# Two buffers for the replaced maxima of a top-k chain, three operand buffers for the mixture layers, and a new table of order

## Chip, cores and metric

One core of a Trainium2 chip runs the whole program. The metric is the device time of one execution in microseconds, as the median of several runs; less is better. The kernel before takes 1180.86 us (median of 3 runs, 1180.18 to 1182.09).

## What is computed

Attention in which each row keeps its 32 largest scores, and behind it two mixture-of-experts layers, all in float32. Cut to what matters:

```python
# q, k, v: (4, 8, 576, 64)
scores = q @ k.T / 8                      # per batch and head: 576 x 576
kth    = the 32nd largest score of a row
scores = where(scores >= kth, scores, -1e9)
attn   = exp(scores - max) / (sum + 1e-9)
x      = (attn @ v), heads side by side   # (2304, 512)
h      = maximum(x @ w_in1, 0)            # (2304, 2048)
x      = (h * h) @ w_out1                 # (2304, 512)
h      = x @ w_in2
out    = (h * clip(h + 3, 0, 6) / 6) @ w_out2
```

## The kernel before

**Tiles.** The 2304 rows are cut, batch by batch, into four blocks of 128 rows and one of 64. A block has eight tiles, one for each head (the block of 64 rows has four, of two heads each, so that they too fill 128 rows). That makes 144 tiles `s` of 128 x 576 scores. `attend(s)` builds the chain of one tile: the scores on TensorE (`qk`, L767, into the one PSUM buffer `s`), their copy to SBUF by ScalarE (`evac`, L773, into one of three buffers `S`), the top-k on VectorE, one bias and the limit (`lowest`, L798), then `below` on ScalarE (L803), `mask` on GpSimd (L806), `expo` on ScalarE (L811), the split of the weights into two float16 parts (`high` L817 on ScalarE, `low` L821 and L822 on GpSimd), a transposing DMA (`flip`), and the product with v on TensorE (`av`, L840, 14 matmuls for a tile). The buffer `S` comes free when `mask` has read it; the next `evac` into that buffer is that of tile `s` + 3.

**The top-k chain.** Seven steps `topk(0)` to `topk(6)` on VectorE: a MAX8 over `S` (L781) gives the eight largest; then three times a MATCH_REPLACE8 (L786) replaces the eight just found by -3e38 and a MAX8 (L789) takes the next eight. The first MATCH_REPLACE8 reads `S` and writes the buffer `W`, the others read and write `W`, and the MAX8s between read `W`. On the chip each MATCH_REPLACE8 is two instructions, of which a MATCH_VALUE_LOAD of the eight values comes first. Each step reads what the step ahead of it wrote. There is one buffer `W`: it is taken by `topk(1)` and comes free behind `topk(6)`, so the next tile can do no more than its first MAX8 until then.

**Mixture layers.** `x_operand(i)` scales and splits a finished block into an operand `hl`; a unit `u` is a block of 128 rows, or two blocks of 64, 18 units in all. For each unit `group(m, u, g)` does, for layer m = 0 and 1 and four groups g: 12 matmuls `up` (L1080), a relu on ScalarE (L1086 or L1088), a square (L1091) or on VectorE a gate (L1094), a split (L1099 on ScalarE, L1102 on GpSimd), a transposing DMA, and 12 matmuls `acc` (L1114). That is 3456 matmuls of 512 columns. The buffer `hl` of a unit is taken by the copy out of PSUM (L912) and comes free behind the last `up` of layer 1; there are four.

**Weights.** Each of the four matrices comes in 16 slabs as 64-bit floats. `w_convert` makes 32-bit ones of them on VectorE (L362 to L365), ScalarE (L408) and GpSimd (L412), TensorE multiplies each slab with itself for a norm (`gram`, L428), and `w_split` splits them in two float16 parts over TensorE and ScalarE (L536 to L545) or ScalarE and GpSimd (L518 to L524). No `up` can start before its matrices are split.

**Order.** Nothing is scheduled at run time: `Plan` writes one list for each engine, and each engine works through its list in order, waiting at the head. `Plan.run` walks through a model of the engines, and whenever an engine is free it takes, of the tasks that are ready and whose buffers are to be had, the one with the smallest key `offset + slope * position`, from the table `PRIO` (L1285 to L1392). So each number of the table, each latency and each buffer count can move instructions on all engines.

Of the kernel before, what the change touches and what calls it, by code (L numbers as in the profile page):

```python
# [9 lines left out]
F32 = mybir.dt.float32  # L10
# [9 lines left out]
P = 128  # L20
# [12 lines left out]
class Plan:  # L33
# [7 lines left out]
    def pool(self, **sizes):  # L41
        for name, n in sizes.items():
            self.pools[name] = list(range(n))
# [91 lines left out]
def tile_topk_attention_moe_moe2(  # L135
# [12 lines left out]
    B, H, S, D = q.shape  # L148
# [40 lines left out]
    def pool(name, n, shape, dtype, where=None):  # L189

        plan.pool(**{name: n})
        size[name] = (shape, dtype, where or sb)
# [20 lines left out]
    acc_t = ps.tile([P, 2, 512], F32, name="acc")  # L213
    plan.pool(acc0=1, acc1=1)
    pool("S", SBUFS, [P, S], F32)
    pool("W", 1, [P, S], F32)
    pool("E", 2, [P, S], F32)
    pool("wc", 2, [P, 2 * S], F16)
    pool("wT", WTB, [P, 2 * S // P, P], F16)
# [6 lines left out]
    pool("f", FBUFS, [P, 512], F32)  # L226
    pool("hl", HBUFS, [P, 2, KD, P], F16)
    pool("ghl", GBUFS, [P, 2, 512], F16)
# [1025 lines left out]
def first_of(order, b):  # L1254
# [6 lines left out]
SBUFS = 3  # L1261
FBUFS = 2
XBUFS = 1
HBUFS = 4
GBUFS = 3
PREFILL = 1
SKV = 'd'
# [15 lines left out]


PRIO = {  # L1285
    "load0": (471.21, 0.193),
    "load1": (618.10, 5.848),
    "load2": (925.04, 0.019),
    "load3": (-584.22, 0.593),
    "conv0": (-88.95, 0.627),  # L1290
    "bits0": (361.28, 2.911),
    "add0": (4977.17, 0.028),
    "gram0": (-831.79, 0.031),
    "conv1": (-93.08, 4.311),
    "bits1": (41.48, 36.796),
    "add1": (368.64, 13.688),
    "gram1": (4879.36, 6.367),
    "conv2": (-80.47, 2.054),
    "bits2": (398.55, 0.019),
    "add2": (449.95, 4.070),  # L1300
    "gram2": (927.27, 0.037),
    "conv3": (-37.62, 1.038),
    "bits3": (-32.80, 0.358),
    "add3": (298.46, 0.239),
    "gram3": (338.67, 0.648),
    "norm": (-1082.21, 0.048),
    "high0": (71.90, 0.086),
    "low0": (72.95, 1.006),
    "scaled0": (205.37, 0.095),
    "rest0": (306.08, 0.054),  # L1310
    "high1": (406.08, 0.677),
    "low1": (-169.41, 49.252),
    "scaled1": (-407.57, 38.073),
    "rest1": (-988.86, 0.160),
    "high2": (983.60, 0.068),
    "low2": (-52.38, 0.243),
    "scaled2": (196.72, 28.830),
    "rest2": (336.50, 0.508),
    "high3": (313.76, 0.250),
    "low3": (-250.55, 0.031),  # L1320
    "scaled3": (307.88, 1.559),
    "rest3": (17.56, 2.177),
    "qsquare": (30.31, 2.898),
    "qtotal": (430.60, 4.982),
    "qscale": (-275.30, 0.171),
    "ksquare": (423.72, 0.406),
    "ktotal": (372.77, 1.000),
    "kscale": (-89.11, 1.034),
    "vsquare": (-201.56, 15.782),
    "vtotal": (-148.39, 5.232),  # L1330
    "vscale": (202.69, 1.991),
    "clear": (4572.71, 0.037),
    "kload": (-15.56, 1.826),
    "vload": (158.91, 2.703),
    "qload": (128.87, 1.164),
    "qhigh": (-47.12, 0.379),
    "qlow": (180.10, 0.411),
    "khigh": (110.60, 0.063),
    "klow": (88.64, 0.053),
    "vhigh": (-0.62, 3.120),  # L1340
    "vlow": (-617.68, 5.745),
    "kflip": (-880.94, 4.825),
    "qscales": (26.46, 0.807),
    "qflip": (39.22, 0.226),
    "qk": (-80.19, 0.810),
    "evac": (-83.75, 1.084),
    "topk": (299.98, 1.000),
    "bias": (-78.63, 7.605),
    "lowest": (300.78, 1.000),
    "below": (-0.40, 4.373),  # L1350
    "mask": (-1424.47, 1.367),
    "expo": (810.67, 1.170),
    "whigh": (-1146.93, 0.851),
    "wlow": (5245.85, 6.690),
    "wflip": (418.75, 3.778),
    "av": (-596.66, 1.207),
    "xinv": (-93.91, 1.674),
    "xscales": (340.01, 0.011),
    "xcopy": (4297.66, 2.864),
    "xflip": (-39.76, 7.585),  # L1360
    "xsquare": (136.44, 0.290),
    "xtotal": (28.37, 7.283),
    "xscale": (146.77, 0.924),
    "xevac": (-46.31, 0.145),
    "xhigh": (-43.97, 0.023),
    "xlow": (-85.79, 0.020),
    "common": (-820.64, 2.732),
    "ysquare": (307.25, 1.077),
    "ytotal": (613.31, 0.179),
    "yflip": (100.03, 2.762),  # L1370
    "yscale": (-497.39, 1.399),
    "yhigh": (330.72, 0.486),
    "ylow": (-206.35, 4.143),
    "whole": (-480.52, 0.870),
    "up0": (4592.97, 2.379),
    "up1": (5118.98, 5.912),
    "relu0": (919.05, 20.673),
    "relu1": (7.31, 2.302),
    "gsquare": (-112.41, 0.730),
    "gate": (109.54, 0.960),  # L1380
    "ghigh0": (83.10, 1.657),
    "ghigh1": (-853.86, 1.145),
    "gflip0": (374.33, 1.182),
    "gflip1": (-496.46, 1.917),
    "glow0": (-26.68, 0.590),
    "glow1": (76.85, 0.449),
    "acc0": (124.81, 0.498),
    "acc1": (788.57, 3.038),
    "oscale": (-125.90, 0.041),
    "oevac": (-4.66, 3.434),  # L1390
    "store": (-2145.32, 6.536),
}  # L1392

_INS = ["q", "k", "v", "moe_w_in", "moe_w_out", "moe2_w_in", "moe2_w_out"]
# [25 lines left out]
```

## Time and profile before

| what | us |
|---|---|
| median of 3 runs | 1180.86 (1180.18 to 1182.09) |
| the profiled execution, its own time | 1179.88 |
| its span in the trace | 1178.0 |
| TensorE (PE) busy | 1025.5, 87% |
| VectorE (DVE) busy | 982.1, 83% |
| ScalarE (ACT) busy | 925.3, 79% |
| GpSimd (POOL) busy | 835.0, 71% |
| MAX8 and MATCH_REPLACE8 of the top-k | 326.3 + 213.8 + 107.9 + 106.9 |
| matmuls of the mixture layers | 453.9 + 443.9 |
| mean granted clock of TensorE | 0.977 of full |

The profile is of one execution. An engine's busy time is the union of its instructions' spans, and spans on VectorE overlap: the next instruction can start before the span of the one ahead has ended. So what an instruction costs on its engine is read from start to start, in the timeline, and not from its duration.

### The profile page before, as it was taken

The numbers are of one execution on the slowest core, as the hardware profiler recorded it, in microseconds if no ns is written. First come the engines' busy times: TensorE is split into PE (matmuls) and PEld (weight loads), VectorE is DVE, ScalarE is ACT, GpSimd is POOL, SyncE is SP. The second block draws the span as 40 slices with busy tenths as digits, with TensorE's granted clock in tenths as the row PEclk, the third lists the DMA queues.
The fourth block names the chain that finished last, engine by engine and source line by source line (L and its number), as shares of the span: only waits on it lengthen the run. The fifth ranks groups of instructions, "written<-read, shape, count | busy, mean of one in ns | idle before, by whom it ended". The sixth has DMA issues, their size and how long they took to land. (4 is left out here: it accounts for less than half of the span.)

```text
span 1178.0 us, 21675 instructions
## 1 busy us (share of the span) xinstructions
PE 1025.5 (87%) x6892; PEld 524.6 (45%) x6892; DVE 982.1 (83%) x2299; ACT 925.3 (79%) x1888; POOL 835.0 (71%) x1112
## 2 busy tenths in 40 slices
PE   2375576879998989899999999999998999999998
PEld 1232333444454545445554545545454444454443
DVE  5999999999875999999999999999698999893110
ACT  7678799689987878889898888889887788776322
POOL 5878868579974768777687887778586778766211
PEclk9997699979999999999999999999999999999999
DMA  9979764664787666568787576667975576665333
GB/s 224 264 248 260 214 145 108 139 114 80 135 167 136 125 109 120 108 126 152 150 172 131 111 131 113 113 129 140 162 116 94 109 127 105 120 92 112 61 65 63
DMA packets 466850, 158.72 MB, mean 135 GB/s; under 512 B 447664, under 2 KB 455856, under 8 KB 466736
## 3 DMA queue, kind: packets, MB, share of 16 engines
q1 hardware_dynamic: 466736, 157.35, 66.2%
q8 instruction: 54, 0.88, 0.3%
q14 instruction: 60, 0.49, 0.1%
HBM read 48.23 MB, written 4.72 MB: 45 GB/s over the span
## 5 line engine op out<-in xcount | busy, mean ns | idle before, releaser
L1114 PE MATMUL acc<-w,ghl 128*128 128x512 f16 x1728 | 453.9, 381 | 12.5 <-DVE xh L277 6.1
L1080 PE MATMUL hb<-w,hl 128*128 128x512 f16 x1728 | 443.9, 380 | 10.4 <-ACT r L1086 5.2
L789 DVE MAX8 m<-W 128x8 f32<-128x576 f32 x432 | 326.3, 755 | 6.1
L1080 PEld LDWEIGHTS <-hl 128*128 128x128 f16 x1728 | 166.9, 99 | 200.2 <-issue 15.9
L1114 PEld LDWEIGHTS <-ghl 128*128 128x128 f16 x1728 | 164.4, 100 | 186.7 <-issue 25.2
L1102 POOL TENSOR_TENSOR gr<-r,gr 128x512 f16<-128x512 f32 x144 | 167.3, 1162 | 97.1 <-ACT gr L1099 79.3
L806 POOL TENSOR_TENSOR E<-S,E 128x576 f32<-128x576 f32 x144 | 204.3, 1419 | 38.2 <-ACT E L803 35.5
L786 DVE MATCH_REPLACE8 W<-m,W 128x576 f32<-128x576 f32 x288 | 213.8, 742 | 0.0
L821 POOL TENSOR_TENSOR wc<-E,wc 128x512 f16<-128x512 f32 x144 | 167.5, 1163 | 50.1 <-ACT wc L817 44.7
L773 ACT ACTIVATE S<-sp 128x576 f32<-128x576 f32 x144 | 93.7, 651 | 50.8 <-POOL E L806 47.9
L803 ACT ACTIVATE E<-S,scalars 128x576 f32<-128x576 f32 x144 | 111.9, 777 | 27.4 <-DVE scalars L798 26.3
L767 PE MATMUL sp<-kT,qT 128*128 128x288 f16 (+1 forms) x640 | 99.6, 296 | 38.5 <-ACT S L773 30.3
L811 ACT ACTIVATE E<-E,scalars,scl 128x576 f32<-128x576 f32 x144 | 125.0, 868 | 1.7 <-POOL E L806 1.5
L781 DVE MAX8 m<-S 128x8 f32<-128x576 f32 x144 | 107.9, 749 | 9.5 <-ACT S L773 9.0
L786 DVE MATCH_REPLACE8 W<-m,S 128x576 f32<-128x576 f32 x144 | 106.9, 742 | 0.0
L1094 DVE SCALAR_TENSOR_TENSOR r<-r,hb 128x512 f32<-128x512 f32 x72 | 48.9, 680 | 68.6 <-ACT r L1088 67.9
L840 PEld LDWEIGHTS <-wT 128*128 128x128 f16 (+1 forms) x2240 | 85.3, 102 | 36.1 <-issue 10.9
L817 ACT ACTIVATE wc<-E 128x576 f16<-128x576 f32 x144 | 98.5, 684 | 0.9
L1099 ACT ACTIVATE gr<-r 128x512 f16<-128x512 f32 x144 | 89.9, 625 | 10.2 <-DVE r L1094 8.6
L767 PEld LDWEIGHTS <-qT 128*128 128x128 f16 (+1 forms) x640 | 56.7, 103 | 86.6 <-issue 54.9
L840 PE MATMUL av<-vv,wT 128*128 128x64 f16 (+1 forms) x2240 | 91.1, 196 | 0.2 <-DMA wT<-wc 0.2
L1088 ACT ACTIVATE r<-hb,bias,scalars 128x512 f32<-128x512 f32 x72 | 55.6, 772 | 42.2 <-PE hb L1080 38.2
(125 smaller groups left out, 1290.0 us busy)
## 6 DMA issues: line engine op xcount, KB each, us to landing
w<-in_moe_w_in_dram SPq DMA_DIRECT2D x32, 512.0 KB, 5.6
w<-in_moe_w_out_dram SPq DMA_DIRECT2D x29, 512.0 KB, 4.5
out_dram<-o SPq DMA_DIRECT2D x16, 256.0 KB, 2.4
qf<-in_q_dram SPq DMA_DIRECT2D x31, 128.0 KB, 2.8
stg<-in_k_dram SPq DMA_DIRECT2D x12, 256.0 KB, 3.1
stg<-in_v_dram SPq DMA_DIRECT2D x12, 256.0 KB, 3.0
wT<-wc SPq DMA_TRANSPOSE x144, 3.3
ghl<-gr SPq DMA_TRANSPOSE x144, 3.2
```

The lines of the kernel that those rows point to most:

```text
L767: nc.tensor.matmul(dst, qT[:, 2 * ((2 * hp + hh) % 4) + a, 0:M], kflat[:, hh * SPAD + c * HALF:hh * SPAD + (c + 1) * HALF], start=a == 0, ...
L781: nc.vector.max(m[:, 0:8], T["S", s])
L786: nc.vector.match_replace(out=T["W", s], in_to_replace=m[:, 8 * c - 8:8 * c], in_values=T["S", s] if c == 1 else T["W", s], imm_value=-3.0e38)
L789: nc.vector.max(m[:, 4 * r:4 * r + 8], T["W", s])
L803: nc.scalar.activation(T["E", s], T["S", s], AF.Relu, bias=T["kb", s], scale=-FAR)
L806: nc.gpsimd.tensor_tensor(T["E", s], T["S", s], T["E", s], op=ALU.subtract)
L811: nc.scalar.activation(T["E", s], T["E", s], AF.Exp, bias=T["nb", s], scale=T["scl", ("q", i, half)][:, hp % 2:hp % 2 + 1], accum_out=T["s ...
L821: nc.gpsimd.tensor_tensor(wc[:, S + TAIL:], e[:, 0:S - TAIL], wc[:, 0:S - TAIL], op=ALU.subtract)
L840: nc.tensor.matmul(out_[cols, t * D:(t + 1) * D], wT[0:kr, a, cols], vv[0:kr, vb, hh, c, :], start=n_ == 0, stop=n_ == len(prods) - 1)
L1080: nc.tensor.matmul(box["h"][0:n, :], hl[:, c, kk, 0:n], wt[2 * m][:, kk * 4 + g, a, :], start=(kk, a, c) == (0, 0, 0), stop=(kk, a, c) == ...
L1102: nc.gpsimd.tensor_tensor(box["gr"][:, 1], box["r"], box["gr"][:, 0], op=ALU.subtract)
L1114: nc.tensor.matmul(o_, gl[d], wt[2 * m + 1][:, f, a, :], start=f == 0 and (a, d) == (0, 0), stop=f == KF - 1 and (a, d) == PRODS[-1])
```

## The change

The pool of `W` has two buffers, the operand pool `hl` three (`HBUFS`), and the table `PRIO` has other numbers in every line.

```diff
-    pool("W", 1, [P, S], F32)
+    pool("W", 2, [P, S], F32)
...
-HBUFS = 4
+HBUFS = 3
...
 PRIO = {
...
-    "topk": (299.98, 1.000),
+    "topk": (4792.55, 5.060),
...
-    "lowest": (300.78, 1.000),
+    "lowest": (407.13, 2.578),
...
 }
```

In SBUF a `W` is 576 float32 numbers in a partition (2304 bytes), an `hl` 2 x 4 x 128 float16 ones (2048 bytes).

The key of a top-k step is `offset + slope * (s + 0.1 r)`, so of two steps that are ready the earlier tile's goes first, in both tables. No instruction is added or removed: the counts on every engine are the same. What the change moves is seen in the lists.

VectorE, in the middle of the program, near the 16th gate; `m_5174` are the maxima of one tile and `W_5244` its buffer, `m_5235` and `W_5336` those of the next. Before:

```order
L789 MAX m_5174<-W_5244 128x8
L781 MAX m_5328<-S_5295 128x8
L786 MATCH_REPLACE W_5336<-m_5235,S_5222 128x576
L798 TENSOR_SCALAR scalars_83<-m_5174 128x1
L789 MAX m_5235<-W_5336 128x8
L261 TENSOR_SCALAR scalars_83<-scalars_83 128x1
L262 TENSOR_SCALAR scalars_83<-scalars_83 128x1
L263 TENSOR_SCALAR scalars_83<-scalars_83 128x1
L786 MATCH_REPLACE W_5336<-m_5235,W_5336 128x576
L789 MAX m_5235<-W_5336 128x8
L786 MATCH_REPLACE W_5336<-m_5235,W_5336 128x576
```

Now, at the same place (the tiles have other numbers):

```order
L786 MATCH_REPLACE W_5178<-m_5144,W_5178 128x576
L786 MATCH_REPLACE W_5254<-m_5216,S_5201 128x576
L789 MAX m_5144<-W_5178 128x8
L789 MAX m_5216<-W_5254 128x8
L798 TENSOR_SCALAR scalars_83<-m_5144 128x1
L781 MAX m_5281<-S_5268 128x8
L786 MATCH_REPLACE W_5254<-m_5216,W_5254 128x576
L1094 SCALAR_TENSOR_TENSOR r_5287<-r_5287,hb_5140 128x512
L789 MAX m_5216<-W_5254 128x8
```

Before, one tile's steps follow each other, and what stands between them is what else happens to be ready. Now a step of another tile stands between them, and two MATCH_REPLACE8s or two MAX8s of different tiles can be neighbours.

ScalarE, at its row 690: the copy of scores into an `S` and the `below` of the tile that had this buffer, three tiles earlier (`S_5803`, `S_5885`, `S_5955` and then `S_6057`). Before:

```order
L803 ACTIVATE E_6037<-S_5803,scalars_83 128x576
L773 ACTIVATE S_6057<-sp_5965 128x576
L811 ACTIVATE E_6037,sums_5723<-E_6037,scalars_83,scl_5377 128x576
L803 ACTIVATE E_6087<-S_5885,scalars_83 128x576
```

Now (`S_5858`, `S_5952`, `S_6016` and then `S_6076`):

```order
L803 ACTIVATE E_6045<-S_5858,scalars_83 128x576
L1099 ACTIVATE gr_6053<-r_5976 128x512
L1088 ACTIVATE r_6062<-hb_6010,bias3_80,scalars_83 128x512
L995 ACTIVATE xh_6070,scalars_83<-acc_90 128x512
L773 ACTIVATE S_6076<-sp_6028 128x576
L811 ACTIVATE E_6045,sums_5696<-E_6045,scalars_83,scl_5336 128x576
```

Before, the copy stands right behind the `below`, whose result the mask on GpSimd still has to use before the buffer is free; now three other instructions stand between.

## Rows read from the trace of the kernel before

**Rows 1.** The page: span, busy time, and PE and DVE in 40 slices.

```profile
span 1178.0 us, 21675 instructions
...
PE 1025.5 (87%) x6892; PEld 524.6 (45%) x6892; DVE 982.1 (83%) x2299; ACT 925.3 (79%) x1888; POOL 835.0 (71%) x1112
...
PE   2375576879998989899999999999998999999998
...
DVE  5999999999875999999999999999698999893110
```

**Rows 2.** Busy time by stage: stretch, length, engines, clock granted, DMA share, GB/s.

```profile
0.00:200.00 200.00, 110.56 (x669) 59.82 (x670) 175.74 (x390) 160.54 (x316) 154.54 (x190) 0.92 0.76 210
200.00:1064.00 864.00, 808.45 (x5689) 416.49 (x5687) 790.55 (x1874) 722.52 (x1497) 648.05 (x889) 0.99 0.68 125
1064.00:1178.00 114.00, 106.54 (x538) 48.26 (x536) 15.78 (x37) 42.24 (x76) 32.43 (x35) 1.00 0.40 75
```

**Rows 3.** Line 1080 (`up`): durations in ns, first and last start in us.

```profile
L1080 PE MATMUL hb<-w,hl x1728: 376/379/634, 207.1 to 1164.4; 128*128 128x512 f16 x192
```

**Rows 4.** Waits of PE from 0 to 200: us in total, times, longest.

```profile
PE acc L428 <- POOL w L412: 41.4, 19, 5.9
```

**Rows 5.** Waits of PE from 200 to 1064.

```profile
PE sp L767 <- ACT S L773: 20.9, 22, 3.0
```

**Rows 6.** Waits of ACT from 200 to 1064.

```profile
ACT S L773 <- POOL E L806: 44.3, 42, 2.8
```

**Rows 7.** Timeline of VectorE, 506 to 516: start, us, instruction, idle before it.

```profile
506.46 0.76 DVE L789 MAX8 m<-W 128x8 f32<-128x576 f32 x1
507.25 0.09 DVE L786 MATCH_VALUE_LOAD W<-m,W 128x8 f32 x1
507.33 0.74 DVE L786 MATCH_REPLACE8 W<-m,W 128x576 f32<-128x576 f32 x1
508.11 0.76 DVE L789 MAX8 m<-W 128x8 f32<-128x576 f32 x1
508.91 0.09 DVE L786 MATCH_VALUE_LOAD W<-m,S 128x8 f32 x1
508.98 0.74 DVE L786 MATCH_REPLACE8 W<-m,S 128x576 f32<-128x576 f32 x1
509.64 0.14 DVE L798 TENSOR_SCALAR scalars<-m 128x1 f32<-128x1 f32 x1
509.70 0.75 DVE L781 MAX8 m<-S 128x8 f32<-128x576 f32 x1
510.37 0.74 DVE L789 MAX8 m<-W 128x8 f32<-128x576 f32 x1
...
514.98 0.74 DVE L781 MAX8 m<-S 128x8 f32<-128x576 f32 x1
515.64 0.07 DVE L786 MATCH_VALUE_LOAD W<-m,S 128x8 f32 x1
```

**Rows 8.** Timeline of all engines, 1055 to 1060: how a buffer `S` passes on.

```profile
1055.74 0.14 DVE L798 TENSOR_SCALAR scalars<-m 128x1 f32<-128x1 f32 x1
...
1055.91 0.77 ACT L803 ACTIVATE E<-S,scalars 128x576 f32<-128x576 f32 x1 [2.07 <-DVE scalars L798]
...
1056.84 1.41 POOL L806 TENSOR_TENSOR E<-S,E 128x576 f32<-128x576 f32 x1 [4.11 <-ACT E L803]
...
1058.27 0.65 ACT L773 ACTIVATE S<-sp 128x576 f32<-128x576 f32 x1 [1.06 <-POOL E L806]
...
1059.04 0.74 DVE L781 MAX8 m<-S 128x8 f32<-128x576 f32 x1
```

**Rows 9.** Timeline of PE, 1084 to 1088: rate of the mixture's matmuls, last `av`.

```profile
1084.83 0.81 PE L1114 MATMUL acc<-w,ghl 128*128 128x512 f16 x3
1085.47 0.81 PE L1080 MATMUL hb<-w,hl 128*128 128x512 f16 x3
...
1087.42 0.57 PE L840 MATMUL av<-vv,wT 128*128 128x64 f16 x14
```

More of the change, by code (lines that the diff above doesn't have):

```diff
@@ L1285 @@
 PRIO = {
[L1286 to L1346, printed above, removed]
-    "topk": (299.98, 1.000),
-    "bias": (-78.63, 7.605),
-    "lowest": (300.78, 1.000),
-    "below": (-0.40, 4.373),
@@ L1351 @@
[L1351 to L1391, printed above, removed]
+    "load0": (892.39, 0.113),
+    "load1": (4535.33, 1.653),
+    "load2": (5326.20, 2.374),
+    "load3": (-586.88, 0.546),
+    "conv0": (-543.99, 2.636),
+    "bits0": (204.34, 20.537),
+    "add0": (849.80, 0.003),
@@ new lines @@
+    "gram0": (862.60, 0.002),
+    "conv1": (839.37, 0.260),
+    "bits1": (-465.19, 2.532),
+    "add1": (13.22, 3.809),
+    "gram1": (-1379.18, 21.153),
+    "conv2": (-1794.75, 7.514),
+    "bits2": (-553.15, 0.013),
+    "add2": (-296.00, 1.020),
+    "gram2": (506.60, 0.338),
+    "conv3": (-209.23, 6.768),
+    "bits3": (131.90, 0.003),
+    "add3": (596.62, 5.872),
+    "gram3": (-498.43, 14.877),
+    "norm": (-2127.51, 0.007),
+    "high0": (250.14, 2.366),
+    "low0": (-31.94, 0.032),
@@ new lines @@
+    "scaled0": (-477.77, 0.008),
+    "rest0": (4866.63, 0.270),
+    "high1": (-522.40, 0.986),
+    "low1": (399.16, 12.656),
+    "scaled1": (-988.99, 226.350),
+    "rest1": (-395.25, 0.044),
+    "high2": (1245.51, 0.133),
+    "low2": (305.26, 11.073),
+    "scaled2": (-495.49, 12.932),
+    "rest2": (-547.16, 0.194),
+    "high3": (382.41, 0.887),
+    "low3": (448.94, 0.100),
+    "scaled3": (-400.04, 101.719),
+    "rest3": (-963.36, 3.154),
+    "qsquare": (-77.46, 3.962),
+    "qtotal": (-846.84, 13.884),
@@ new lines @@
+    "qscale": (-1998.02, 0.009),
+    "ksquare": (-428.04, 0.593),
+    "ktotal": (-2026.48, 4.644),
+    "kscale": (994.85, 0.035),
+    "vsquare": (445.78, 5.343),
+    "vtotal": (-307.08, 1.199),
+    "vscale": (142.77, 19.208),
+    "clear": (504.75, 0.003),
+    "kload": (468.74, 0.940),
+    "vload": (-415.70, 3.785),
+    "qload": (-2303.64, 11.797),
+    "qhigh": (-291.82, 0.287),
+    "qlow": (262.90, 4.026),
+    "khigh": (-84.38, 3.778),
+    "klow": (-538.78, 1.932),
+    "vhigh": (-2296.80, 1.406),
@@ new lines @@
+    "vlow": (-713.21, 3.468),
+    "kflip": (-507.41, 0.095),
+    "qscales": (-566.46, 9.630),
+    "qflip": (-1167.30, 0.144),
+    "qk": (-203.08, 1.514),
+    "evac": (-351.22, 0.272),
+    "topk": (4792.55, 5.060),
+    "bias": (134.82, 12.545),
+    "lowest": (407.13, 2.578),
+    "below": (17.22, 6.283),
+    "mask": (-2028.49, 0.090),
+    "expo": (568.95, 0.075),
+    "whigh": (190.28, 0.516),
+    "wlow": (575.89, 5.224),
+    "wflip": (76.55, 7.911),
+    "av": (-211.24, 3.589),
+    "xinv": (12.21, 4.724),
@@ new lines @@
+    "xscales": (349.83, 0.027),
+    "xcopy": (19.46, 0.471),
+    "xflip": (21.42, 16.269),
+    "xsquare": (191.49, 0.021),
+    "xtotal": (47.58, 1.206),
+    "xscale": (-2267.32, 0.038),
+    "xevac": (116.73, 0.011),
+    "xhigh": (-83.18, 0.002),
+    "xlow": (339.70, 0.004),
+    "common": (-227.86, 3.010),
+    "ysquare": (-92.64, 1.879),
+    "ytotal": (589.77, 1.776),
+    "yflip": (240.08, 0.010),
+    "yscale": (302.83, 0.389),
+    "yhigh": (-437.82, 1.811),
+    "ylow": (458.57, 5.597),
@@ new lines @@
+    "whole": (-155.58, 4.349),
+    "up0": (4603.62, 0.306),
+    "up1": (4837.12, 11.722),
+    "relu0": (747.75, 6.852),
+    "relu1": (-542.89, 4.150),
+    "gsquare": (-853.85, 0.276),
+    "gate": (238.37, 16.365),
+    "ghigh0": (444.20, 0.284),
+    "ghigh1": (-164.30, 0.457),
+    "gflip0": (-1001.68, 0.264),
+    "gflip1": (337.67, 0.456),
+    "glow0": (-2315.66, 0.043),
+    "glow1": (665.29, 1.035),
+    "acc0": (-84.30, 7.190),
+    "acc1": (636.44, 2.170),
+    "oscale": (-971.27, 0.012),
@@ L1392 @@
+    "oevac": (-518.46, 6.203),
+    "store": (-1981.38, 18.713),
 }
```

## Prediction

> **What bounds the kernel now.** I read the page first [rows 1]. TensorE (PE) is busy 1025.5 us of 1178.0 and VectorE (DVE) 982.1; no other engine comes near. The slices show that this average hides three stages: PE has digits of 2 to 8 at the start and 9 from then on; DVE has 9 almost from the start and falls to 3, 1, 1, 0 in the last four slices. The table by stage [rows 2] gives the stages numbers. Up to 200 us PE works 110.6 of 200 us and DVE 175.7: the weights are being converted, and the first `up` matmul starts at 207.1 [rows 3]. From 200 to 1064, when the last av matmuls draw near, PE works 808.5 of 864 us (55.6 idle) and DVE 790.6 (73.4 idle): the two are nearly level, and what makes one wait can be the other. From 1064 on PE works 106.5 of 114 us on mixture layers that are left over, and DVE has almost nothing to do. So the kernel's time is the start of the mixture, plus PE's work behind it, plus what PE idles in between. A change on VectorE can only win what PE idles, not what VectorE saves.
>
> How much of PE's idle time depends on VectorE is seen in the waits. In the middle stage 20.9 us of 55.6 are spent at the scores matmuls (`qk`), which wait until ScalarE has copied the scores of the tile ahead into an `S` [rows 5]. ScalarE in its turn waits 44.3 us for GpSimd's mask to give an `S` back [rows 6], and the mask comes behind `lowest`, the last step of a top-k [rows 8]. So this chain goes at VectorE's pace. In the first stage PE's largest wait is another one: 41.4 us for GpSimd's part of the conversion [rows 4].
>
> **Term 1: what VectorE saves.** In the timeline a step that reads what the step just ahead has written starts later than one that does not [rows 7]. MAX8 at 506.46 and the MATCH_VALUE_LOAD that takes its result at 507.25: 0.79 us. MATCH_REPLACE8 at 507.33 and the MAX8 on its result at 508.11: 0.78. MAX8 at 508.11 and the load for the next tile at 508.91: 0.80, because that tile must write the single `W` that the MAX8 still reads. Without such a tie: MATCH_REPLACE8 at 508.98 to `lowest` of another tile at 509.64, 0.66; MAX8 at 514.98 to a load at 515.64, 0.66. And the case that the change makes common, a step whose own source is two places ahead: MAX8 over `S` at 509.70, then at 510.37 the MAX8 over the `W` that was written at 508.98, 0.67. A tie to the direct neighbour thus costs 0.13 (MAX8 to MATCH_REPLACE8) or 0.12 (the reverse), a tie one place farther 0.01.
>
> Counted over VectorE's whole list, before has 231 pairs MAX8 to MATCH_REPLACE8 and 179 pairs MATCH_REPLACE8 to MAX8 that are tied so; the changed list has 40 and 35. That saves 191 x 0.13 = 24.8 and 144 x 0.12 = 17.3, together 42 us of VectorE's time. The changed list has one kind of neighbours that no row of before shows: 116 times a MATCH_REPLACE8 directly behind one of another tile. Its load could start 0.66 behind, as everything untied behind a MATCH_REPLACE8 does, or 0.80 as in the slowest row; a gain is excluded, since 0.66 is the least that any row has behind it. I take 0.66, the row of the same instruction; the other end costs 116 x 0.14 = 16 us, and the saving would be 26.
>
> The Trainium skill speaks against this term: "VectorE: DVE Perf Modes", section "The DRAIN you can't avoid", says that behind every operation the next one waits until the pipeline is empty, and that dropping semaphores doesn't help. By it the saving would be nothing and the sum that of the second rival below.
>
> **Term 2: the start, -3 us.** Of the 418 tied steps of the old list only 27 stand in its first 400 rows, since conversions of weights already fill the gaps there; the new list has 3. 24 x 0.125 = 3 us by which VectorE can be through with that part sooner. The conversion's wait for GpSimd [rows 4] is not touched.
>
> **Term 3: the middle, -14 us.** Some 39 us of VectorE's 42 fall behind the start. VectorE's idle time there isn't made larger by the change: lists have the same instructions. PE can take of it what it now idles for VectorE's sake, 20.9 us at most [rows 5]. I take two thirds, 14 us: once VectorE is some 4% faster, PE is the bound and the rest of these waits is jitter in ScalarE's and GpSimd's queues, as is the remainder of the 55.6 us (relus, gates, splits), which I leave as it is. The order of ScalarE supports the direction: the copy into an `S` stands directly behind the `below` of the tile that had it, or with up to two instructions between, 52 times of 141 before and 37 times now.
>
> **Term 4: mixture work moved forward, -4 us.** In PE's list 150 mixture matmuls stand ahead of the end of the 24th tile's av before, 189 now. At 0.65 us for three [rows 9] the 39 are 8.4 us of work in a stretch where PE isn't full. Part of it is what term 2 already counts, and the table may have been paid for it elsewhere, so I take half.
>
> **Edits at nothing.** The third fewer `hl`: the copy of a unit waits for the last `up` of the unit three before. In PE's list that matmul stands ahead of the last av which the same copy needs anyway, for all units but one (there 39 matmuls behind, 8.4 us if nothing hides it), and PE goes through its list in order. The tail: behind the last av, which runs at 1087.4 in before [rows 9], the new list has 423 mixture matmuls and the old 375; 48 more are 10.4 us, but the same 48 are missing ahead of it. That costs nothing as long as PE is full on both sides; if it isn't, up to 10.4.
>
> **Sum.** The profiled execution took 1179.9. 1179.9 - 3 - 14 - 4 = 1159. The median of the runs shown, 1180.86, lies 1.0 above that execution, so I predict **1160 us**.
>
> **Rivals.**
> *PE's idle time goes almost altogether.* If relus and gates wait because ScalarE is held up at the `S` copies, as ScalarE's 44.3 us there suggest [rows 6], the other waits shrink too. 40 of the 55.6 us, 3 at the start and 2 more of term 4 than I took: 1181 - 45 = 1136. Against it: in before PE is already at 9 in nearly every slice.
> *The saving doesn't arrive.* Either the next instruction on VectorE has to wait for the pipeline whatever stands ahead of it, the rule named above; then terms 1 to 3 fall and term 4 alone is left, 1177. I give that 0.04, since the rows have 0.66 beside 0.79 for the same instructions [rows 7]. Or the saving is real and PE's waits at `qk` move to the next station, to GpSimd (busy 75% in the middle stage [rows 2]): then a third of term 3 stays, 1181 - 3 - 5 - 2 = 1171; 0.15.
> *Slower: three buffers `S` for two chains.* A tile now shares VectorE with another one and holds its `S` for twice as long. Once its `lowest` is through, the buffer passes by way of below, mask and copy to the MAX8 of the tile three later: 1055.74 to 1059.04, 3.3 us at the quickest [rows 8]. If the list puts that MAX8 sooner than the path can deliver, it stands at the head of VectorE's queue and all behind it wait. With 0.5 us lost at each of 125 tiles, 62 us against 42 saved, the kernel is 20 us slower, 1200; it decides from 0.34 us a tile on. Against it: between `lowest` and that MAX8 the old list had at most five top-k instructions in 59 cases of 141, the new one in 15, so the list gives the path more time than before.
>
> **How the numbers follow.** The forecast with its spread (1150 to 1168) gets 0.50, the full gain 0.18, the small one 0.15, no saving 0.04, slower 0.13. The range leaves out the ends of the first and the last: 1136 to 1183. A measurement of this kernel can tell 0.2% from no change, some 2.4 us. Faster than that: 0.50 + 0.18 + 0.15 and half of the 0.04, 0.84; the same 0.04, from the no-saving case and the mildest of the slower one; slower 0.12.
>
> **What would show it.** In the timeline of VectorE steps of two tiles should alternate 0.66 apart, and the load between two MATCH_REPLACE8s start 0.66 behind the first, not 0.80. The idle time of PE from the first `up` to the last av should fall by about 15 us, the wait at `qk` for the copy most, and the first `up` start 2 to 8 us sooner. I am wrong if MAX8 over `S` becomes VectorE's largest wait, if `up` starts later than 207, or if PE's idle time stays and only VectorE's grows.

## The result, and the profile after

The changed kernel takes **1162.6 us** (median of 4 runs, 1161.5 to 1164.9) beside 1181.2 of the kernel before (now median of 4 runs, 1180.2 to 1182.1): a ratio of 0.9845, 95% interval 0.9828 to 0.9863, 18.6 us less. Forecast were 1160, with 1136 to 1183 as range. The profiled execution took 1161.47 us with a span of 1159.8, against 1179.88 and 1178.0.

The page after: span, busy time, PE and DVE in 40 slices, as in [rows 1].

```profile
span 1159.8 us, 21591 instructions
...
PE 1024.0 (88%) x6892; PEld 522.6 (45%) x6892; DVE 949.3 (82%) x2299; ACT 923.9 (80%) x1888; POOL 832.8 (72%) x1112
...
PE   2475486888999989999999999999899999999998
...
DVE  4999999998967998999999999998599999970110
```

VectorE's busy time is 32.8 us shorter with the same 2299 instructions; that of the other engines stays within 2.3 us. Busy time by stage, as in [rows 2], without the last stage:

```profile
0.00:200.00 200.00, 113.12 (x663) 60.30 (x664) 174.28 (x392) 158.04 (x309) 151.17 (x181) 0.91 0.78 216
200.00:1064.00 864.00, 820.83 (x5815) 421.75 (x5815) 763.26 (x1881) 735.73 (x1533) 661.55 (x913) 1.00 0.71 126
```

In the middle stage PE idles 43.2 us where it idled 55.6, and VectorE idles 100.7 where it idled 73.4. VectorE's longest wait there is now that of the gates (L1094) for ScalarE's relu, 27.2 us where it was 2.7:

```profile
DVE r L1094 <- ACT r L1088: 27.2, 12, 17.0
```

The 17.0 is one wait, which ends at 1059.9, when VectorE has no top-k step left in its list.

The timeline of VectorE after, in the same part of the program as [rows 7] (x2 is two neighbours merged):

```profile
502.78 0.74 DVE L786 MATCH_REPLACE8 W<-m,S 128x576 f32<-128x576 f32 x1
503.44 0.08 DVE L786 MATCH_VALUE_LOAD W<-m,W 128x8 f32 x1
503.51 0.74 DVE L786 MATCH_REPLACE8 W<-m,W 128x576 f32<-128x576 f32 x1
504.17 1.41 DVE L789 MAX8 m<-W 128x8 f32<-128x576 f32 x2
505.50 0.07 DVE L786 MATCH_VALUE_LOAD W<-m,W 128x8 f32 x1
```

Two tiles alternate, and here no step starts later than 0.67 behind its neighbour. The open case, a load behind another tile's MATCH_REPLACE8, is 502.78 to 503.44: 0.66. All 116 such pairs of the trace lie between 0.659 and 0.661.

The waits after, of PE and then of ACT, from 200 to 1064, as in [rows 5, 6]:

```profile
PE sp L767 <- ACT S L773: 9.1, 12, 2.2
PE acc L1114 <- ACT xh L995: 7.9, 8, 2.5
```

```profile
ACT S L773 <- POOL E L806: 24.3, 30, 1.8
```

Two rows of before that the following compares with, of ACT and of DVE, from 200 to 1064:

```profile
ACT E L803 <- DVE scalars L798: 24.1, 23, 3.3
```

```profile
DVE m L781 <- ACT S L773: 9.0, 15, 1.8
```

PE's wait at `qk` has more than halved, ScalarE's wait for the mask nearly so. New at the second place is PE's wait for the squares of the first layer's result (L995): 7.9 us, 2.2 before. ScalarE's `below`, which waited 24.1 us for `lowest` before, now waits 6.1 for it, and 11.7 for GpSimd's `low` of an earlier tile to give an `E` back.

Where the 18.2 us of span went, PE's account (span = busy + idle; cut at 200 us and at the last av, 1087 before and 1061 after; "busy" in the last row is working time, the others are idle):

| stretch | PE idle before | after |
|---|---|---|
| 0 to 200 | 200 - 110.6 = 89.4 | 86.9 |
| 200 to the last av | 887 - 831.1 = 55.9 | 861 - 817.8 = 43.2 |
| from the last av on | 91 - 83.8 = 7.2 | 98.8 - 93.1 = 5.7 |
| PE busy, whole span | 1025.5 | 1024.0 |

The differences are 2.5, 12.7 and 1.5 us of idle time and 1.5 us of busy time. The matmuls are the same, and the mean granted clock of TensorE was 0.977 in the profiled execution before and 0.981 after.

The first `up` starts at 207.8 (207.1 before):

```profile
207.79 1.02 PE L1080 MATMUL hb<-w,hl 128*128 128x512 f16 x4 [0.68 <-ACT w L545]
```

### The profile page after: what moved, and what is told of

Its sections match the earlier page's. It is cut to its first block, busy times and chain, and to the rows that moved or that the text cites. A ratio compares the mean times of both kernels' runs of the same rounds, so it can differ in the third digit from the quotient of the medians.

```text
span 1159.8 us, 21591 instructions
## 1 busy us (share of the span) xinstructions
PE 1024.0 (88%) x6892; PEld 522.6 (45%) x6892; DVE 949.3 (82%) x2299; ACT 923.9 (80%) x1888; POOL 832.8 (72%) x1112
## 5 line engine op out<-in xcount | busy, mean ns | idle before, releaser
L789 DVE MAX8 m<-W 128x8 f32<-128x576 f32 x432 | 314.7, 749 | 1.2
L803 ACT ACTIVATE E<-S,scalars 128x576 f32<-128x576 f32 x144 | 111.5, 775 | 22.6 <-POOL wc L822 11.7
L1094 DVE SCALAR_TENSOR_TENSOR r<-r,hb 128x512 f32<-128x512 f32 x72 | 49.0, 681 | 87.0 <-ACT r L1088 85.9
L1099 ACT ACTIVATE gr<-r 128x512 f16<-128x512 f32 x144 | 89.9, 625 | 11.8 <-DVE r L1094 8.7
```

The lines of the kernel that those rows point to most:

```text
L789: nc.vector.max(m[:, 4 * r:4 * r + 8], T["W", s])
L803: nc.scalar.activation(T["E", s], T["S", s], AF.Relu, bias=T["kb", s], scale=-FAR)
```

## Experiments

All ratios are against the kernel before, run beside them on the same chip; its median was 1182.0 in the first group, 1182.3 in the second and 1183.0 in the third.

**The theory** at first: the gain comes from VectorE's untied steps, as far as PE idles for VectorE. **Rivals**: the new table made it; three `hl` cost something.

### One half of the change at a time

`new_table_w1_h3` has the new table with one `W`, `new_table_w1_h4` with four `hl` as well (so the table alone), `old_table_w2_h3` the buffers with the old table. (No run has two `W` with four `hl`, so three `hl` were not undone alone.)

```diff
 new_table_w1_h3 (from the changed kernel)
-    pool("W", 2, [P, S], F32)
+    pool("W", 1, [P, S], F32)
 new_table_w1_h4 (besides)
-HBUFS = 3
+HBUFS = 4
 old_table_w2_h3 (from the kernel before)
-    pool("W", 1, [P, S], F32)
+    pool("W", 2, [P, S], F32)
-HBUFS = 4
+HBUFS = 3
```

> The changed kernel with one buffer W again (three hl and the new table stay). VectorE's list then has 198 pairs MAX8 to MATCH_REPLACE8 and 251 pairs MATCH_REPLACE8 to MAX8, all tied, where the changed kernel has 40 and 35 tied ones: 158 x 0.13 + 216 x 0.12 = 46 us more on VectorE. Theory (the gain comes by VectorE's ties, as far as PE idles for them): the gain is gone, 1176 to 1190 us, and PE's wait at qk for the copy into S is back at 18 us or more from 200 to 1064. Rival (the new table made the gain, the second W little of it): 1162 to 1168 us, and that wait stays near 9 us.

> The new table alone: one W, four hl. VectorE's list has 198 and 249 tied pairs. Theory (ties): as with three hl, 1176 to 1190 us, and within 3 us of that run, since the third fewer hl costs nothing. Rival (table): 1162 to 1168. Second rival (three hl hold the mixture up): 8 us or more faster than the run with one W and three hl.

> The buffers alone: two W, three hl, the old table. VectorE's list has 175 + 145 pairs of MAX8 and MATCH_REPLACE8 and 82 pairs of two MATCH_REPLACE8, of which 151 pairs are tied (357 in the kernel before, 75 in the changed one, counted the same way): about 26 us of VectorE's time saved. Theory (ties): most of the gain is there, 1160 to 1172 us. Rival (table): no gain without the new table, 1176 to 1190 us.

| run | us | ratio and interval |
|---|---|---|
| new_table_w1_h3 | 1230.0 | 1.0399 (1.0381 to 1.0417) |
| new_table_w1_h4 | 1224.5 | 1.0352 (1.0333 to 1.0372) |
| old_table_w2_h3 | 1201.8 | 1.0164 (1.0149 to 1.0179) |

None came out as either side said: each half alone makes the kernel slower, by 43 to 48 and by 20 us, and the halves together make it faster by 19. PE's wait at `qk` in `new_table_w1_h3` is 35.2 us. The slower times don't come from the start: the first `up` of these three runs starts at 177.6, 177.9 and 180.2 us, some 27 to 30 sooner than before. A list is made by the table and the buffer counts together, so a table that suits one count of `W` can give a list that suits the other badly. Waits of PE and of DVE, from 200 to 1064, in `old_table_w2_h3`:

```profile
PE sp L767 <- ACT S L773: 20.2, 27, 4.0
```

```profile
DVE m L781 <- ACT S L773: 28.1, 18, 4.5
```

VectorE is mostly untied there (busy 957.8 us), and what it saved went into waits at the head of its list: 28.1 us for the copy into an `S`, 9.0 in the kernel before. This already speaks against the theory as I had put it: less time on VectorE is no gain by itself. But each of these runs reshuffles every list, so they tell no part of the change from another. The next runs keep the lists.

### VectorE's time alone, lists kept

`before_shorter` and `after_shorter` cut the columns of each top-k step, of the MATCH_REPLACE8s as of the MAX8s; `after_padded` puts five instructions of one column between the steps.

```diff
 before_shorter, after_shorter
-                nc.vector.max(m[:, 0:8], T["S", s])
+                nc.vector.max(m[:, 0:8], T["S", s][:, 0:534])
...
 after_padded
         def topk(r):
+            if 0 < r < 6: nc.vector.tensor_scalar(padt[:, r:r + 1], ones32[:, 0:1], 1.0, None, op0=ALU.mult)
```

> The kernel before with its lists as they are, but each of the seven top-k steps looks at 534 of a row's 576 columns, so the last 42 scores of a row are left out of the search. At 0.96 columns a ns that is 7 x 42 / 0.96 = 0.31 us less for a tile, 44 us of VectorE's time, as much as the change took away by untying steps, with no step moved and one buffer W. Theory (VectorE's saved time counts as far as PE idles for it): 1160 to 1170 us, PE's wait at qk for the copy into S falls by 8 us or more. Rival (the new order made the gain, not VectorE's time): 1177 us or more.

> The changed kernel with the same 534 columns: 44 us less on VectorE once more. Theory (PE is now the bound, little of its idle time is VectorE's): 3 to 12 us faster than the changed kernel, 1150 to 1160. Rival (VectorE bounds it still): the full gain of the change again, 16 us or more, below 1147.

> The changed kernel with the same lists, and five instructions of one column (0.06 us each, start to start) put between the steps of each top-k: 144 x 0.30 = 43 us given back to VectorE. Theory: much of the gain is gone, 1173 to 1185 us. Rival (order alone made the gain, VectorE has room): 1166 or less.

| run | us | ratio and interval |
|---|---|---|
| before_shorter | 1178.3 | 0.9962 (0.9946 to 0.9977) |
| after_shorter | 1160.6 | 0.9807 (0.9788 to 0.9826) |
| after_padded | 1173.3 | 0.9928 (0.9906 to 0.9950) |

The first is the important miss. The saving of the change, made in the old lists, is worth 4 us and not 12 to 20. PE's waits and VectorE's in `before_shorter`, from 200 to 1064:

```profile
PE sp L767 <- ACT S L773: 21.8, 24, 2.9
```

```profile
DVE m L781 <- ACT S L773: 19.9, 33, 2.0
```

```profile
ACT S L773 <- POOL E L806: 45.3, 47, 2.8
```

PE waits as long at `qk` as before (20.9), ScalarE as long for the mask (44.3), and VectorE waits 19.9 us for the same copies instead of 9.0. So in the old lists the copies into `S` don't come at VectorE's pace alone; a faster VectorE mostly waits for them too.

In the new lists VectorE's time does count: the padding costs 1173.3 - 1162.6 = 10.7 us (9.8 by the ratios), as the theory's lower edge said. But it gives back less than the 43 us of the expectation. The padding instructions also part most of the steps that were still tied, and start to start VectorE's work for the top-k grows by some 34 us; its busy time grows by 34.0 as well, from 949.3 to 983.3. Of the 45 us that the change saves, then, about a quarter is not given back. The wait of ScalarE for the mask stays where the changed kernel has it (24.3):

```profile
ACT S L773 <- POOL E L806: 24.6, 29, 1.7
```

Another 44 us less are worth little: 2.0 us by the medians, 0.0038 x 1182 = 4.5 by the ratios. That run, too, lies just outside what the theory said (1150 to 1160).

### The turn of the three S, lists kept

If not VectorE, then the way of an `S` from `lowest` by below, mask and copy back to VectorE [rows 8] sets the pace of the copies. These three take the kernel before with the same lists and change only where buffers lie: `W` in two places and `hl` in three; or `S` in four and `hl` in three; or the latter with 534 columns.

```diff
 lists_kept_s4_h3 (the pools of the plan stay 3 and 4)
-            T["S", s] = take("S")
+            T["S", s] = sb.tile([P, S], F32, tag=f"S{s % 4}", name="S", bufs=1)
-                T["hl", u] = take("hl")
+                T["hl", u] = sb.tile([P, 2, KD, P], F16, tag=f"hl{u % 3}", name="hl", bufs=1)
 lists_kept_w2_h3 (hl as above)
-                    T["W", s] = take("W")
+                    T["W", s] = sb.tile([P, S], F32, tag=f"W{s % 2}", name="W", bufs=1)
```

> The kernel before with every engine's list as it was, instruction by instruction, but the buffers of the change: W in two places in turn, hl in three. That unties the 55 places where the next tile's first MATCH_REPLACE8 had to wait for the MAX8 on the only W: 7 us of VectorE's time. Theory now (in the old lists VectorE's time hardly counts, and the buffers alone do nothing): within 3 us of the kernel before, 1178 to 1184. Rival 1 (three hl hold the mixture up): slower by 5 us or more. Rival 2 (the second W itself makes the gain): 1172 or less.

> The kernel before with every list as it was, one W, hl in three places and S in four instead of three, so that a copy of scores no longer waits for the mask of the tile three before, but of the one four before. Theory now (in the old lists PE's wait at qk is the turn of the three S by way of below, mask and copy, and not VectorE's pace): ScalarE's wait for the mask at the copy falls from 44 to under 12 us, PE's wait at qk from 21 to under 8, and the time to 1165 to 1174. Rival (VectorE's pace sets that wait; the buffer only passes it on): ScalarE's wait falls, but the time stays at 1178 or more.

> The same with four S, and the top-k over 534 of 576 columns, so the last 42 scores of a row are left out of the search and VectorE has 44 us less to do. With three S that was worth 4 us. Theory now (the turn of S hid VectorE's gain): 10 us or more faster than the run with four S and all columns, 1150 to 1163. Rival (VectorE's time doesn't count in the old lists for another reason): within 5 us of it.

| run | us | ratio and interval |
|---|---|---|
| lists_kept_w2_h3 | 1182.5 | 1.0002 (0.9991 to 1.0013) |
| lists_kept_s4_h3 | 1177.6 | 0.9955 (0.9939 to 0.9970) |
| lists_kept_s4_shorter | 1169.1 | 0.9883 (0.9856 to 0.9909) |

The buffers of the change, without its lists, do nothing together: no gain of the second `W` is left, and no loss by three `hl` (that one undoes the other isn't excluded, since no run of the old lists changes only one of them). A fourth `S` is worth 5.4 us, less than the 9 to 18 I expected; the time lies at the edge of the rival's, 1178. Waits of PE, and of ACT, from 200 to 1064, in `lists_kept_s4_h3`:

```profile
PE sp L767 <- ACT S L773: 10.9, 17, 3.1
```

```profile
ACT E L803 <- DVE scalars L798: 34.0, 32, 3.9
```

PE's wait at `qk` is halved (under 8 was expected). ScalarE no longer waits for the mask at the copy (44.3 us before, not among its longest waits now), but 34.0 us instead of 24.1 for `lowest`: with the turn of `S` eased, VectorE's pace comes forward. With 534 columns that wait falls to 22.7, and VectorE's 44 us are worth 1177.6 - 1169.1 = 8.6 us in the same old lists, twice the 4 of `before_shorter`, a little short of the 10 I expected. That the turn of `S` hid part of VectorE's gain fits this, but the difference of some 4 us is as wide as the intervals of these runs taken together, so it is likely rather than shown.

### TensorE's time, lists kept

```diff
 before_fewer_mm, after_fewer_mm
-            for a, d in PRODS:
+            for a, d in PRODS[:3 - m]:
...
```

> The changed kernel with one of the three acc products of layer 1 left out, so that layer is less exact: 288 matmuls x 0.216 = 62 us less on TensorE, lists otherwise the same. Theory (PE is the bound): 35 to 60 us faster than the changed kernel, 1103 to 1128, until VectorE becomes the bound. Rival (VectorE bounds it still): 1145 or more.

> The kernel before with one of the three acc products of layer 1 left out, so that layer is less exact: 288 matmuls x 0.216 = 62 us less on TensorE, lists otherwise the same. In the changed kernel that gave 20 us. Theory now (the old lists hang on the turn of S and on VectorE more than on PE): 5 to 18 us faster than the kernel before, 1163 to 1176. Rival (PE bounds both alike): 20 us or more.

| run | us | ratio and interval |
|---|---|---|
| before_fewer_mm | 1169.0 | 0.9880 (0.9865 to 0.9895) |
| after_fewer_mm | 1143.1 | 0.9660 (0.9644 to 0.9676) |

The 288 matmuls left out, some 62 us at 0.216 each (PE's busy time falls by 49 us from the kernel before and by 47 from the changed one), give 14 us before and 19.5 after (21.9 by the ratios). After, that is not the 35 to 60 that a bound by TensorE would give, but a little more than the 17.6 at most that the rival's 1145 stood for; before, it lies in the 5 to 18 expected. PE's longest wait in `after_fewer_mm`, from 200 to 1064:

```profile
PE sp L767 <- ACT S L773: 20.4, 34, 2.2
```

It stands at `qk` 20.4 us where the changed kernel had 9.1: a faster PE waits for the copies into `S` again. In `before_fewer_mm` the same wait is 38.3 us, 20.9 before. So the changed kernel hangs on TensorE more than the old one does, and still on the copies into `S` as well.

## Why the prediction was right, and where its reasons weren't

**The sum.** 1160 forecast, 1162.6 measured; of 21 us expected 18.6 came. The terms fit less well than the sum. By PE's account the start gave 2.5 us of idle time (3 forecast), the stretch from 200 us to the last av 12.7 (terms 3 and 4 together: 18), and 3.0 came from what the forecast had at nothing: 1.5 of idle time in the tail and 1.5 of PE's busy time. That the sum is so near is in part luck. (The chances listed for "faster" add up to 0.85, not 0.84.)

**Term 1, VectorE's saving: right.** 42 us forecast. Summed over the timeline, the time that ties cost is 57 us in before and 12 after, 45 less. Of it 52 and 10 us are steps that start more than 0.66 behind the direct neighbour to which they are tied; the rest, 5 and 2, are steps with only a short instruction between them and their source, which the forecast had not counted. The pair that no row had shown costs nothing extra. The rule of the Trainium skill ("VectorE: DVE Perf Modes", "The DRAIN you can't avoid") that the next operation waits for the pipeline to empty, whatever the semaphores, doesn't hold for these instructions: 0.66 untied against 0.78 to 0.80 tied. The same section adds that an operation which isn't held starts earlier, and that half agrees with the trace: an untied step starts 0.66 behind one whose span is 0.74.

**Term 2, the start 3 us sooner: wrong.** The first `up` starts at 207.8, 0.7 later, which by the letter is one of the signs of being wrong that I had named ("later than 207"). That sign could tell nothing: before itself starts at 207.1, and the runs that keep its lists start between 207.9 and 211.1. In both kernels PE idles 0.7 us ahead of the first `up` for a split of the weights on ScalarE (L545), and not for VectorE. PE's longest wait up to 200 us, for GpSimd's part of the conversion, is 39.0 us (41.4 before), nearly untouched as I had said; PE's idle time there fell by 2.5 us all the same.

**Term 3, the middle: the size near, the reason wrong.** 14 us forecast, 12.4 measured (55.6 to 43.2), about 2 of it term 4's; the wait at `qk`, where I had put it, fell by 11.8. The step that failed is the sentence that this chain goes at VectorE's pace. `before_shorter` shows that it doesn't in the old lists: there VectorE's 44 us are worth 4 us and `qk` waits as long as before. Two things held it: the turn of three `S`, and VectorE. Taking away one alone gives 4 or 5 us, both together 13.9 (`lists_kept_s4_shorter`). PE's idle time from 200 us to the last av, in the profiled execution of each, says the same without PE's busy time, which varies by 4 us between these executions:

| run | PE idle, us |
|---|---|
| before | 55.9 |
| lists_kept_w2_h3 | 58.2 |
| before_shorter | 54.2 |
| lists_kept_s4_h3 | 50.1 |
| lists_kept_s4_shorter | 44.9 |
| after | 43.2 |
| after_padded | 49.4 |
| after_shorter | 41.6 |

The change saves VectorE's time by two `W` and the order that goes with them, and the order may ease the turn of `S` as well: the copy stands farther behind the `below` that it depends on. With some 34 of VectorE's 45 us given back, the new lists are still 8 to 9 us faster than the old ones (`after_padded`), and the other 10 us are VectorE's. In proportion the rest of the 45 would cost another 3 us or so, an estimate from that one run, and leave 5 or 6 to the order. That this share is the turn of `S` is likely: ScalarE's wait for the mask is 44 to 46 us in the runs with the old lists and three `S`, whatever VectorE has to do, and 24 to 25 in the new lists, with VectorE's work cut, as it is or padded. But it isn't shown: no run has the new lists with another number of `S`. The forecast also took VectorE's idle time as not made larger; it went from 73.4 to 100.7 us.

**Term 4, mixture work moved forward: it moved, but it is no term of its own.** From 200 to 300 us the trace has 166 + 120 mixture matmuls, 153 + 114 before: 19 x 0.216 = 4.1 us, 4 forecast. PE's idle time in that stretch fell by only 2.1 us, from 15.9 to 13.8, and these 2.1 are part of the 12.4 of term 3; the forecast counted them beside it.

**The tail: as forecast.** The last av starts at 1060.7 instead of 1087.4 and has 99.1 us behind it instead of 90.6. These 8.5 us are work that PE would have done before; it is no emptier there than it was (idle 5.7 us, 7.2 before).

**"PE is the bound": too simple.** I took two thirds of the wait at `qk` because PE would then be full. It is not: with 288 matmuls less on PE, some 62 us, only 19.5 come through.

**The rivals.** The slower one, three buffers `S` for two chains, named the right resource, but in the new order ScalarE waits less for it and not more (24.3 us for the mask, 44.3 before); what the rival feared may show in `old_table_w2_h3`, where the second `W` comes without the order made for it: VectorE waits 28.1 us for the copies and the kernel is 20 us slower, though that run moves other things too.

## What to carry to other kernels

Where each engine works through a list made beforehand, a faster engine can just wait longer at the head of its list, as VectorE did here in `before_shorter`: test what its time is worth with the list kept (shorten or pad its instructions) before crediting a saving to it, and read from the trace how much time the padding really gave back. A buffer, and the table that orders the work, belong together: try them as one change, for each alone can lose what both together gain. Before calling a wait the pace of the engine at the end of a chain, give the buffer that is handed around one more place and see whether the wait stays.

## What the runs showed of the chip that I had not expected

A load of match values directly behind another tile's MATCH_REPLACE8 starts 0.66 us behind it, like any untied instruction, in all 116 places. A step with another top-k step between it and its source starts 0.66 to 0.68 behind that neighbour, as untied ones do. But a short instruction in between is not enough. With only a `lowest` between, the step still starts about 0.78 behind its source, as late as directly behind it, here 521.31 to 522.08 in before:

```profile
521.31 0.74 DVE L786 MATCH_REPLACE8 W<-m,S 128x576 f32<-128x576 f32 x1
521.97 0.14 DVE L798 TENSOR_SCALAR scalars<-m 128x1 f32<-128x1 f32 x1
522.08 0.76 DVE L789 MAX8 m<-W 128x8 f32<-128x576 f32 x1
```

In before that is so in all 87 places with one short instruction between (0.74 to 0.79). So in these traces it is its source that holds a tied step back, and an instruction between hides that only if it takes as long as another tile's step.
